# Moving weight loads, U^T loads and six dense blocks around the handover of DK in a fused SSM and dense backward kernel

## The chip, the core and the metric

The kernel runs on one core of a Trainium2 chip. The metric is the device time of one execution in microseconds, as the median of several runs. A NeuronCore has five engines with queues of their own: TensorE (PE, matmuls and transposes, with its weight loads shown apart as PEld), VectorE (DVE), ScalarE (ACT), GpSimd (POOL) and SyncE (SP). SP, ACT and POOL also issue DMA transfers. An engine takes its instructions in the order of its queue; an instruction that waits holds up all that stand behind it there.

## The reference

The kernel computes a forward pass and all its gradients for a gated mix of two branches over one sequence (L = 2048, D = 448):

```python
def _fwd_reference(A_u, ..., B_w1, B_b1, B_w2, B_b2, gate_w):
    x = A_u
    g = _sigmoid((x * gate_w).sum(-1, keepdims=True))
    a = _A_ref(x, A_A_re, ..., A_log_dt, A_Dskip)   # S4: K = Re(sum_n C P dB), y = FFT conv of u with K, + u * Dskip
    b = _B_ref(x, B_w1, B_b1, B_w2, B_b2)           # relu(x w1 + b1)^2 w2 + b2, F = 1792
    return g * a + (1 - g) * b
...
_out, _vjp = jax.vjp(_f, A_u, A_A_re, ..., gate_w)
_grads = _vjp(grad_out)
return (_out, *_grads)
```

The S4 branch's kernel K is a sum over 256 complex modes per channel of powers of exp(dt A) up to 2047, rounded positions included. Its gradient, called DK here, comes from a correlation of u with g * grad_out.

## The kernel before

**Until about 215 us.** The FFT-like stages turn u and g * grad_out into spectra, multiply them, and go back through a first inverse stage (`K.inv1p`), which writes its result to the DRAM scratch `hd[0]`. `K.load_hs(hd[0], q, hss[q], True)` brings it back as four tiles of 128 x 3584 in bf16 (two in tag D16, two in tag P14), with half of the issues on SP and half on ACT. 128 and more small matmuls (L713, weights `Ew`) sum it into DK, held in PSUM tiles N0 to N3 and F.

**The handover of DK.** ACT copies the PSUM tiles to SBUF (L717 to L719). Twelve stores and one for a single row write them to the DRAM scratch `dk_d`, in turns from SP and POOL (L726, L728). Then SP and POOL each reload the whole of DK, once into partitions 0 to 63 and once into 64 to 127 (L733, L735), in the layout that the chunk loop wants. A reload waits for the stores.

**The chunk loop** (`for c in range(NCH + 1)`, 14 chunks of 32 channels, and one round more) builds tables of powers of the modes and uses them in both directions. For chunk c: `seeds_x`, `build_x` and `build_y` (DVE, L773 to L777 and L784 to L787) double tables X and Y step by step, with multipliers that ACT expands (`expand_x`, L807 and L808; `expand_y`, L812 and L814); `kgen` and `k_out` (L844, L852) multiply X and Y into the forward kernel K; `tables_t` and `turn_yt` transpose X and Y through PE, with ACT copies (L871, L883), and `load_yt` does so by DMA for some. `dk_chunk(c)` (ACT, L895 and L896) cuts chunk c's part of DK into `DKs`. In the round after, `back_z(c - 1, ...)` multiplies Y's transposes with `DKs` (L913, "Z", into PSUM tile F, copied by ACT in L917), and `back_p` multiplies Z with X's tables on DVE (L933) and sums with a selection matrix on PE (L942). Tile F has one buffer, so a Z group needs the copy of the one before.

**The dense layers** run beside the loop. `hidden(lb, jp, banks, ring)` computes two blocks of 128 rows of relu(x w1 + b1)^2 for a quarter `lb` of the sequence: eight matmuls (L584, L587) into two PSUM tiles from `banks`, two relus (L589) and a square (L591 or L594) on ACT, and a store of the relu from POOL (L595). Seven `jp` make a quarter. It needs w1 (`w1w`, tag U16, three loads on SP, L697 and L700) and a quarter of U^T (`UTb`, in SB, `load_ut` on POOL, L568). `project` (L1021) multiplies by w2 (`w2n`, tag D16, one load on POOL, L1029) and needs all seven. Then come the transposes of w1 and w2, and `row_block` (L1084 to L1097) for the backward of the dense branch; its products on DVE (L1096) stand in the same queue as the loop's. After the loop K goes through DRAM (`k_d`, `gd[2]`) and the FFT stages for the outputs.

**What sets the order.** The program is written as one text; a scheduler orders each engine's queue at compile time by the place in the text and by when operands are ready in its own model. It may put an instruction ahead of others written before it. Inside `with tc.issue_after(x.ins):` each instruction on x's engine stays behind x in that engine's queue; it does not wait for x's end.

Of the kernel before, what the change touches and what calls it, by code (L numbers as in the profile page):

```python
# [19 lines left out]
P = 128  # L20
L, D, N, F = 2048, 448, 256, 1792
# [313 lines left out]
def kernel(ctx, tc, A_u, A_A_re, A_A_im, A_B_re, A_B_im, A_C_re, A_C_im, A_log_dt, A_Dskip,  # L335
# [3 lines left out]
    nc = tc.nc  # L339
# [6 lines left out]
    def dscr(name, n, dt=bf16):  # L346
        return nc.dram_tensor(name, (n,), dt, kind="Internal")
# [8 lines left out]
    dk_d = dscr("dk_d", 769 * D)  # L356
# [109 lines left out]
    NT = ["N0", "N1", "N2", "N3", "X", "S"]  # L466
# [100 lines left out]
    def load_ut(lb):  # L567
        G_.dma_start(UTb[lb % 2].rearrange("p a l -> p (a l)"), bass.AP(tensor=UT_d, offset=lb * P * 2048, ap=[[2048, P], [1, 2048]]))  # L568

    def hsq(j):  # L570
        return SB[:, 4096 + 512 * j:4608 + 512 * j] if j < 13 else w2v[:, 6272:6784]

    def hidden(lb, jp, banks, ring):
        nonlocal nti, rxi
        ub = UTb[lb % 2]
        rx = ring[rxi % len(ring)]
        rxi += 1
        pss = []
        for j in (2 * jp, 2 * jp + 1):
            ps = K.ps(banks[nti % len(banks)], [P, 512])  # L580
            nti += 1
            pss.append(ps)
            for dt in range(DT - 1):
                T_.matmul(ps[:], lhsT=w1w[:, dt, j * P:j * P + P], rhs=ub[:, dt], start=(dt == 0), stop=False, skip_group_check=True)  # L584
        for k in range(2):
            h, j = slice(64 * k, 64 * k + 64), 2 * jp + k
            T_.matmul(pss[k][:], lhsT=w1w[h, 3, j * P:j * P + P], rhs=ub[h, 3], start=False, stop=True, tile_position=(64 * k, 0), skip_group_check=True)  # L587
        for k in range(2):
            S.activation(rx[:, 512 * k:512 * k + 512], pss[k][:], ACT.Relu, bias=b1_f[:, 2 * jp + k:2 * jp + k + 1])  # L589
        if jp < 6:  # L590
            S.activation(SB[:, 4096 + 1024 * jp:5120 + 1024 * jp], rx, ACT.Square)  # L591
        else:
            for k in range(2):
                S.activation(hsq(12 + k), rx[:, 512 * k:512 * k + 512], ACT.Square)  # L594
        G_.dma_start(bass.AP(tensor=rT_d, offset=2 * jp * P * L + 512 * lb, ap=[[L, P], [P * L, 2], [1, 512]]), rx.rearrange("p (k l) -> p k l", k=2))  # L595
# [96 lines left out]
    for q in range(4):  # L692
        lhs = K.load_hs(hd[0], q, hss[q], True)
    w1v = K.t("U16", [P, 8192])
    w1w = w1v[:, 0:7168].rearrange("p (a f) -> p a f", a=DT)
    with tc.issue_after(lhs.ins):
        nc.sync.dma_start(w1w[:, 0:3], bass.AP(tensor=B_w1.tensor, offset=B_w1.offset, ap=[[F, P], [P * F, 3], [1, F]]))  # L697
    for h in range(2):
        with tc.issue_after(lhs.ins):
            nc.sync.dma_start(w1w[64 * h:64 * h + 64, 3], bass.AP(tensor=B_w1.tensor, offset=B_w1.offset + 384 * F, ap=[[F, 64], [1, F]]))  # L700
    KB = K.t("K28", [P, 14336])
    DK = KB[:, 0:VA * D].rearrange("p (a d) -> p a d", d=D)
    G_.memset(KB[:, 12 * D:VA * D].bitcast(fp32), 0.0)
# [18 lines left out]
    ldk = {}  # L722
    for (a0, na, r0, st_, src) in pieces:
        for al in range(na):
            qe = (nc.sync, G_)[n_ % 2]
            ldk[n_ % 2] = qe.dma_start(bass.AP(tensor=dk_d, offset=(r0 + al) * D, ap=[[st_ * na * D, 16 // st_], [16 * na * D, 4], [1, D]]), src[al::na])  # L726
            n_ += 1
    ldk[n_ % 2] = (nc.sync, G_)[n_ % 2].dma_start(bass.AP(tensor=dk_d, offset=768 * D, ap=[[D, 1], [1, D]]), stB[0:1, 1])  # L728
    for cpy in range(2):
        qe = (nc.sync, G_)[cpy]  # L730
        with tc.issue_after(ldk[cpy].ins):
            for (a0, na, r0, st_, _) in pieces:
                qe.dma_start(DK[64 * cpy:64 * cpy + 64, a0:a0 + na].rearrange("p a d -> p (a d)"),  # L733
                             bass.AP(tensor=dk_d, offset=r0 * D, ap=[[na * D, 64], [1, na * D]]))
            qe.dma_start(DK[64 * cpy:64 * cpy + 1, 12], bass.AP(tensor=dk_d, offset=768 * D, ap=[[D, 1], [1, D]]))  # L735


    YA = K.t("Y16", [P, W2, 2, 64])
# [2 lines left out]
    XWs = [XB[:, 4096 * k:4096 * k + 4096].rearrange("p (t w a r) -> p t w a r", t=2, w=W2, a=NA) for k in range(2)]  # L741
    for k in range(2):
        mx = G_.memset(XB[:, 4096 * k:4096 * k + 4096].bitcast(fp32), 0.0)
    with tc.issue_after(mx.ins):
        load_ut(0)
        load_ut(1)
    Fv = K.t("F17", [P, 8704])
    Vt = Fv[:, 0:4096]
    PRY = Fv[:, 4096:5376].rearrange("p (l w t d) -> p l w t d", l=5, t=2, d=2)
# [43 lines left out]
    def seeds_x(c):  # L793
        V.tensor_copy(XWs[c % 2].rearrange("p t w a r -> p (t w) (a r)")[:, :, 0:4], rx_[c][:, 0:512].rearrange("p (x e) -> p x e", e=4))

    def load_rx(c):
        rx_[c] = K.t("recx", [P, 1024])
        (G_ if c == 1 else nc.sync).dma_start(rx_[c][:], bass.AP(tensor=rec_d, offset=c * P * RS, ap=[[RS, P], [1, 1024]]))
# [17 lines left out]
    def build_x(c):  # L816
        for (s0, st, dst, n, k) in ((0, 1, 2, 2, 0), (0, 2, 4, 2, 1), (0, 4, 6, 2, 2), (0, 4, 8, 2, 3), (6, 1, 10, 3, 3)):
            last = step_x(XWs[c % 2], s0, st, dst, n, k)
        return last
# [66 lines left out]
    def load_yt(c, g):  # L886
        nonlocal yi
        YT = (YTr[yi % 4] if yi % 4 < 3 else P2[:, 2048:4096]).rearrange("p (h i n) -> p h i n", h=2, i=CW)
        yi += 1
        nc.sync.dma_start_transpose(out=YT.rearrange("p h i n -> p (h i) n"), in_=Ys[c % 2][:, 16 * g:16 * g + 16].rearrange("p w t b -> p (w t b)"))  # L890
        return YT
# [6 lines left out]
    def back_z(c, YTs, gs):  # L898

        nonlocal zi  # L900
        cc = c % GC
        DKc = DKs[:, c % 2]
        zb = Zr[zi % 2].rearrange("p (s t g n) -> p s t g n", t=2, s=2, g=2)
        zi += 1
        for gg, g in enumerate(gs):
            psz = K.psF()
            for s in range(2):
                for par in (1, 0):
                    for ii in range(4):
                        i = 2 * ii + par  # L910
                        m = (1 + par) * NA
                        for t in range(2):
                            T_.matmul(psz[32 * ii:32 * ii + m, t, 256 * s:256 * s + 256],  # L913
                                      lhsT=DKc[64 * t:64 * t + 64, s, g, 2 * ii:2 * ii + 1 + par].rearrange("p i a -> p (i a)"),
                                      rhs=YTs[g][64 * t:64 * t + 64, :, i, :], start=True, stop=True, tile_position=(64 * t, 32 * ii),
                                      skip_group_check=True)
            S.copy(zb[:, :, :, gg].rearrange("p s t n -> p t s n"), psz[:].rearrange("p t (s n) -> p t s n", s=2))  # L917
        return zb
# [46 lines left out]
    for c in range(NCH + 1):  # L965
        z01 = z23 = None
        if c < NCH:
            with tc.issue_after(ay.ins) if ay is not None else nullcontext():
                seeds_x(c)
            ax = build_x(c)  # L970
            if c + 1 < NCH:
                load_rx(c + 1)
            XTs[c] = [tables_t(c, 0)]
            YTs[c] = []
        if c > 0:
            z01 = back_z(c - 1, YTs[c - 1], (0, 1))
        if c < NCH:
            XTs[c].append(tables_t(c, 1))
        if c > 0:
            z23 = back_z(c - 1, YTs[c - 1], (2, 3))  # L980
        for half in range(2):
            if c < NCH:
                ay = build_y(c, half, ax if half == 0 else ap or ay)
                if half == 1:
                    k_out(c, kgen(c))
                for g in (2 * half, 2 * half + 1):
                    YTs[c].append(turn_yt(c, g, ("S", "N3")) if c == 0 else turn_yt(c, g) if g == 3 or c == NCH - 1 else load_yt(c, g))
                if c + 1 < NCH:
                    if half == 0:
                        lry = load_ry(c + 1)  # L990
                        lry1 = lry if c == 0 else lry1
                        expand_x(c + 1)
                        if c == 0:
                            expand_y(1, 0, 4)
                    elif c == 0:
                        expand_y(1, 4, 5)
                    else:
                        expand_y(c + 1)
                if half == 0:
                    dk_chunk(c)  # L1000
            ap = None
            if c > 0:
                ap = back_p(c - 1, XTs[c - 1][half], (z01, z23)[half], (2 * half, 2 * half + 1), ay if c < NCH else None)
        if c == 0:
            for jp in range(6):
                hidden(0, jp, NT[4:6], [w1v[:, 7168:8192], Fv[:, 2048:3072], Fv[:, 3072:4096]])

    ring = [w1v[:, 7168:8192], Fv[:, 2048:3072], Fv[:, 3072:4096], P2[:, 0:1024], P2[:, 1024:2048]]
    ni = 0
# [15 lines left out]

    w2v = K.t("D16", [P, 8192])
    w2n = w2v[:, 0:FT * D].rearrange("p (j d) -> p j d", d=D)
    with tc.issue_after(lry1.ins):
        G_.dma_start(w2n, bass.AP(tensor=B_w2.tensor, offset=B_w2.offset, ap=[[D, P], [P * D, FT], [1, D]]))  # L1029
    hidden(0, 6, NT[0:3], ring)  # L1030
    for lb in range(4):
# [410 lines left out]
```

## Time and profile before

| | us |
|---|---|
| Median of 5 runs (lowest, highest) | 951.65 (943.29, 961.45) |
| Profiled execution, own time | 951.03 |
| Its span, first to last instruction | 948.9 |
| Granted TensorE clock, mean | 0.841 of full |

| Stretch, us | What runs | DVE busy | ACT busy | PE busy |
|---|---|---|---|---|
| 209 to 236 | DK's last sums and handover; chunk 1's tables | 19.5 | 13.4 | 17.6 |
| 236 to 263 | first Z, hidden of the first quarter | 12.0 | 26.0 | 22.5 |
| 316 to 342 | one chunk in the middle of the loop | 25.3 | 21.2 | 21.2 |
| 650 to 700 | after the loop | 16.5 | 19.9 | 37.6 of 50 |

Times in the profile are microseconds from the start of the span. In a line of the timeline stand start, duration, engine, line, operation, output and input tile; in square brackets the idle time of the engine before it and what ended that. In the list of waits stand the time in all, how often, and the longest. In the DMA issues stand the size of one and the median time from issue to landing.

### The profile page before, as it was taken

How to read it: one execution, taken by the hardware profiler on the slowest of the kernel's cores; microseconds unless marked ns; L12 is line 12 of the kernel's file. 1: busy time of each engine (PE TensorE's matmuls, PEld its weight loads, DVE VectorE, ACT ScalarE, POOL GpSimd, SP SyncE). 2: the span in 40 equal slices, each digit the busy share in tenths (PEclk: the TensorE clock that was granted, in tenths of full speed). 3: DMA queues.
4: the chain of work that ended last, by engine and by line, in shares of the span. 5: the costliest groups of instructions: out<-in, count | busy, mean ns of one | idle time of the engine just before them, and what ended most of it. 6: DMA issues, size and time to landing. Idle time of an engine off the chain costs nothing. (4 is left out here: it accounts for less than half of the span.)

```text
span 948.9 us, 19001 instructions
## 1 busy us (share of the span) xinstructions
PE 709.3 (75%) x7657; PEld 341.7 (36%) x7657; DVE 671.0 (71%) x1152; ACT 587.0 (62%) x936; POOL 191.8 (20%) x327
## 2 busy tenths in 40 slices
PE   3335574636978888887898887988968789767975
PEld 1112221214344443433463442543323245423443
DVE  4388985696399999999987899845249571297700
ACT  3346757825998868788776764655337636437543
POOL 2141000112202121121211311232300022433310
PEclk9677665767969998999958997989979979868998
DMA  9987385796626667445844776379989994879431
GB/s 190 261 246 266 128 341 232 300 313 195 148 59 128 152 141 140 107 106 120 193 89 122 217 156 160 90 186 284 383 300 283 297 290 134 236 225 282 146 107 44
DMA packets 161887, 184.98 MB, mean 195 GB/s; under 512 B 90963, under 2 KB 137464, under 8 KB 160872
## 3 DMA queue, kind: packets, MB, share of 16 engines
q1 hardware_dynamic: 111958, 82.38, 35.3%
q0 software_dynamic: 20480, 61.51, 20.1%
q10 hardware_dynamic: 29362, 39.88, 12.7%
q8 instruction: 60, 0.98, 0.4%
q14 instruction: 27, 0.22, 0.1%
HBM read 90.58 MB, written 73.13 MB: 173 GB/s over the span
## 5 line engine op out<-in xcount | busy, mean ns | idle before, releaser
L933 DVE TENSOR_TENSOR P<-R 128x2048 bf16<-128x2048 bf16 x42 | 49.5, 1218 | 24.2 <-ACT R L917 20.8
L1159 PEld LDWEIGHTS <-S 128*128 128x128 bf16 x448 | 43.8, 103 | 61.3 <-issue 18.4
L917 ACT CAST R<-psF 128x1024 bf16<-128x1024 f32 x56 | 57.3, 1024 | 13.3 <-PE psF L913 13.3
L1021 PE MATMUL psN<-D,S 128*128 128x448 bf16 x208 | 50.5, 374 | 6.4 <-ACT S L591 6.3
L1159 PE MATMUL psF<-U,S 128*128 128x448 bf16 x224 | 50.4, 374 | 2.4 <-ACT S L1154 2.4
L584 PE MATMUL psN<-S,U 128*128 128x512 bf16 x132 | 41.5, 434 | 8.8 <-ACT F L589 4.4
L913 PE MATMUL psF<-R,S 64*32 64x256 bf16 (+1 forms) x1344 | 38.6, 302 | 10.5 <-DMA R<-Y 4.2
L1084 PE MATMUL psN<-S,U 128*128 128x512 bf16 x126 | 39.1, 432 | 6.9 <-ACT D L1089 6.9
L773 DVE TENSOR_TENSOR X<-X,F 128x512 bf16<-128x512 bf16 (+1 forms) x70 | 37.5, 536 | 4.5 <-ACT F L807 2.6
L784 DVE TENSOR_TENSOR K<-K,F 128x2048 bf16<-128x2048 bf16 (+3 forms) x42 | 36.4, 866 | 5.1 <-ACT F L812 3.5
L1153 PEld LDWEIGHTS <-S 128*128 128x128 bf16 x448 | 29.6, 102 | 27.0 <-issue 10.1
L207 DVE CAST K<-psN 128x448 bf16<-128x448 f32 x36 | 21.6, 620 | 24.8 <-PE psN L255 24.6
L785 DVE TENSOR_TENSOR F<-K,F 128x2048 bf16<-128x2048 bf16 (+3 forms) x42 | 35.9, 854 | 3.3 <-ACT F L814 3.3
L1097 POOL DMA_DIRECT2D dhT_d<-D x28 | 20.1, 720 | 88.8 <-DVE D L1096 88.5
L784 DVE TENSOR_TENSOR Y<-Y,F 128x2048 bf16<-128x2048 bf16 (+3 forms) x42 | 36.3, 864 | 1.6
L787 DVE TENSOR_TENSOR K<-K,F 128x2048 bf16<-128x2048 bf16 (+3 forms) x42 | 36.4, 866 | 1.3
L774 DVE TENSOR_TENSOR F<-X,F 128x512 bf16<-128x512 bf16 (+1 forms) x70 | 36.9, 527 | 0.6
L787 DVE TENSOR_TENSOR Y<-Y,F 128x2048 bf16<-128x2048 bf16 (+3 forms) x42 | 36.3, 865 | 1.3
L785 DVE TENSOR_TENSOR F<-Y,F 128x2048 bf16<-128x2048 bf16 (+3 forms) x42 | 35.9, 855 | 0.3 <-ACT F L814 0.3
L1021 PE MATMUL psN<-S,D 128*128 128x448 bf16 x168 | 35.7, 361 | 0.0
L1354 DVE SCALAR_TENSOR_TENSOR F<-psN,Y 128x448 bf16<-128x448 f32 x16 | 9.9, 617 | 36.4 <-PE psN L329 36.4
L913 PEld LDWEIGHTS <-S 64*16 64x16 bf16 (+1 forms) x1792 | 22.4, 91 | 34.5 <-issue 26.7
(378 smaller groups left out, 1942.8 us busy)
## 6 DMA issues: line engine op xcount, KB each, us to landing
sp<-K ACTq DMA_DIRECT2D x8, 896.0 KB, 5.8
hd<-st ACTq DMA_DIRECT2D x16, 448.0 KB, 3.2
dhT_d<-D POOLq DMA_DIRECT2D x28, 256.0 KB, 5.3
R<-sp SPq DMA_DIRECT2D x8, 896.0 KB, 9.9
S<-rT_d POOLq DMA_DIRECT2D x14, 512.0 KB, 5.3
R<-hd SPq DMA_DIRECT2D x16, 448.0 KB, 6.7
S<-dhT_d POOLq DMA_DIRECT2D x14, 512.0 KB, 4.6
rec_d<-F ACTq DMA_DIRECT2D x2, 1920.0 KB, 9.1
```

Source lines behind the costliest of these rows:

```text
L584: T_.matmul(ps[:], lhsT=w1w[:, dt, j * P:j * P + P], rhs=ub[:, dt], start=(dt == 0), stop=False, skip_group_check=True)
L773: V.tensor_tensor(out=hi4, in0=lo, in1=bcast_dims(pr, [0, (None, n), 1]), op=ALU.mult)
L774: V.tensor_tensor(out=Vv.rearrange("p (x a r) -> p x a r", x=2 * W2, r=2), in0=lo, in1=bcast_dims(pi, [0, (None, n), 1]), op=ALU.mult)
L784: V.tensor_tensor(out=hi, in0=lo, in1=bcast_dims(pr, [0, (None, n // 2), 1]), op=ALU.mult)
L785: V.tensor_tensor(out=Vv.rearrange("p (x a q) -> p x a q", x=rows, q=2), in0=lo, in1=bcast_dims(pi, [0, (None, n // 2), 1]), op=ALU.mult)
L787: return V.tensor_tensor(out=T4[:, :, :, n:2 * n], in0=T4[:, :, :, n:2 * n], in1=V4, op=ALU.add)
L913: T_.matmul(psz[32 * ii:32 * ii + m, t, 256 * s:256 * s + 256], lhsT=DKc[64 * t:64 * t + 64, s, g, 2 * ii:2 * ii + 1 + par].rearrange("p i ...
L917: S.copy(zb[:, :, :, gg].rearrange("p s t n -> p t s n"), psz[:].rearrange("p t (s n) -> p t s n", s=2))
L933: lastp = V.tensor_tensor(out=pr.rearrange("p s t g n -> p s t (g n)"), in0=zv, in1=(xb if r == 0 else rev_dim(xb, 2)), op=ALU.mult)
L1021: lastm = T_.matmul(ps[:, 0:D], lhsT=hblk[j][:, P * tt:P * tt + P], rhs=ws[:, j, :], start=(w == 1 and j == 0), stop=(j == FT - 1))
L1084: T_.matmul(ps[:], lhsT=w2Tw[:, jp, dt, j % 2], rhs=dblk[:, dt], start=(dt == 0), stop=False, skip_group_check=True)
L1159: lastm = T_.matmul(ps[:, 0:width], lhsT=hh[:, t, :], rhs=(DB2[:, t, :] if w == 0 else U[:, t, 0:D + 1]), start=(t == 0), stop=(t == LT - 1))
```

## The change

Five edits. The three loads of w1 stand behind SP's last store of DK instead of behind the last load of `hd[0]`; the two loads of U^T stand behind POOL's last store of DK instead of behind a memset of X's buffers; the load of w2 stands behind POOL's last reload of DK instead of behind the load of chunk 1's Y record. `dk_chunk(0)` is written in the second half of chunk 0's round, not the first (the other chunks' stay). The six calls `hidden(0, 0)` to `hidden(0, 5)` are written in round c = 1, behind both `back_z` of chunk 0, instead of at the end of round c = 0, and use PSUM tiles N0, N1, N2 in place of X and S.

```diff
@@ -693,11 +693,6 @@
     w1v = K.t("U16", [P, 8192])
     w1w = w1v[:, 0:7168].rearrange("p (a f) -> p a f", a=DT)
-    with tc.issue_after(lhs.ins):
-        nc.sync.dma_start(w1w[:, 0:3], bass.AP(tensor=B_w1.tensor, offset=B_w1.offset, ap=[[F, P], [P * F, 3], [1, F]]))
-    for h in range(2):
-        with tc.issue_after(lhs.ins):
-            nc.sync.dma_start(w1w[64 * h:64 * h + 64, 3], bass.AP(tensor=B_w1.tensor, offset=B_w1.offset + 384 * F, ap=[[F, 64], [1, F]]))
...
     ldk[n_ % 2] = (nc.sync, G_)[n_ % 2].dma_start(bass.AP(tensor=dk_d, offset=768 * D, ap=[[D, 1], [1, D]]), stB[0:1, 1])
+    with tc.issue_after(ldk[0].ins):
+        nc.sync.dma_start(w1w[:, 0:3], bass.AP(tensor=B_w1.tensor, offset=B_w1.offset, ap=[[F, P], [P * F, 3], [1, F]]))
+        for h in range(2):
+            nc.sync.dma_start(w1w[64 * h:64 * h + 64, 3], bass.AP(tensor=B_w1.tensor, offset=B_w1.offset + 384 * F, ap=[[F, 64], [1, F]]))
+    with tc.issue_after(ldk[1].ins):
+        load_ut(0)
+        load_ut(1)
     for cpy in range(2):
...
-            qe.dma_start(DK[64 * cpy:64 * cpy + 1, 12], bass.AP(tensor=dk_d, offset=768 * D, ap=[[D, 1], [1, D]]))
+            lrk = qe.dma_start(DK[64 * cpy:64 * cpy + 1, 12], bass.AP(tensor=dk_d, offset=768 * D, ap=[[D, 1], [1, D]]))
...
-    with tc.issue_after(mx.ins):
-        load_ut(0)
-        load_ut(1)
...
             z23 = back_z(c - 1, YTs[c - 1], (2, 3))
+        if c == 1:
+            for jp in range(6):
+                hidden(0, jp, NT[0:3], [w1v[:, 7168:8192], Fv[:, 2048:3072], Fv[:, 3072:4096]])
         for half in range(2):
...
-                if half == 0:
+                if half == (1 if c == 0 else 0):
                     dk_chunk(c)
...
-        if c == 0:
-            for jp in range(6):
-                hidden(0, jp, NT[4:6], [w1v[:, 7168:8192], Fv[:, 2048:3072], Fv[:, 3072:4096]])
...
-    with tc.issue_after(lry1.ins):
+    with tc.issue_after(lrk.ins):
         G_.dma_start(w2n, bass.AP(tensor=B_w2.tensor, offset=B_w2.offset, ap=[[D, P], [P * D, FT], [1, D]]))
```

## The prediction

> **What bounds the kernel now.** I read the busy table first, then the windows around the change, then the waits of VectorE (DVE) and ScalarE (ACT) there, the timeline, and last the DMA issues. The busy table says only that TensorE and VectorE are both near three quarters.
>
> ```profile
> PE 709.3 (75%) x7657; PEld 341.7 (36%) x7657; DVE 671.0 (71%) x1152; ACT 587.0 (62%) x936; POOL 191.8 (20%) x327
> ```
>
> The windows show where which engine counts.
>
> ```profile
> core 0: us, PE busy (x) PEld busy (x) DVE busy (x) ACT busy (x) POOL busy (x), PEclk, DMA share, GB/s
> 209.00:236.00 27.00, 17.56 (x297) 12.59 (x298) 19.51 (x33) 13.41 (x21) 8.05 (x14) 0.83 0.75 221
> 236.00:263.00 27.00, 22.46 (x283) 9.95 (x284) 12.04 (x12) 26.04 (x38) 4.91 (x7) 0.91 0.63 145
> 316.00:342.00 26.00, 21.17 (x356) 10.76 (x339) 25.28 (x39) 21.21 (x31) 3.47 (x6) 0.93 0.60 138
> 498.00:524.00 26.00, 21.47 (x230) 8.46 (x208) 19.84 (x24) 18.69 (x27) 5.09 (x9) 0.83 0.54 134
> ```
>
> A chunk of the loop takes 26 us, and DVE is busy for 25.3 of them: the loop goes at DVE's pace. Only where the loop starts (236 to 263) does DVE work 12 of 27 us; there ACT is full (26.0) and PE nearly so. Later, at 498, DVE waits again, on the dense layers. The waits of DVE and ACT between 209 and 260 name the holes:
>
> ```profile
> DVE P L933 <- ACT R L917: 12.9, 1, 12.9
> ACT S L895 <- DMA K<-dk_d: 5.5, 1, 5.5
> DVE K L784 <- ACT F L812: 3.5, 1, 3.5
> DVE F L785 <- ACT F L814: 3.3, 1, 3.3
> ```
>
> The timeline tells their story:
>
> ```profile
> 233.97 0.89 ACT L895 COPY S<-K 128x416 bf16<-128x416 bf16 x1 [5.50 <-DMA K<-dk_d]
> 236.09 1.23 DVE L784 TENSOR_TENSOR K<-K,F 128x2048 bf16<-128x2048 bf16 x1 [3.49 <-ACT F L812]
> 242.17 0.69 ACT L589 ACTIVATE U<-psX,b_f 128x512 bf16<-128x512 f32 x1
> 245.93 1.04 ACT L917 CAST R<-psF 128x1024 bf16<-128x1024 f32 x1
> 251.52 1.07 ACT L917 CAST R<-psF 128x1024 bf16<-128x1024 f32 x1
> 252.63 2.36 DVE L933 TENSOR_TENSOR P<-R 128x2048 bf16<-128x2048 bf16 x2 [12.92 <-ACT R L917]
> ```
>
> ACT stands at dk_chunk(0) (L895) until DK has landed; behind it in ACT's queue stand expand_y(1, 4, 5) and the copies of turn_yt, and DVE waits 3.5 us for the first. Then PE and ACT alternate between the hidden blocks (L584, L589, L591) and the first Z (L913, L917): two Z copies are 5.6 us apart, and DVE gets its first product 12.9 us late. The DMA issues of 188 to 240 show why DK lands at 233.9:
>
> ```profile
> P<-hd SPq DMA_DIRECT2D x2, 448.0 KB, 15.1
> U<-in_B_w_dram SPq DMA_DIRECT2D x2, 224.0 KB, 16.2
> D<-in_B_w_dram POOLq DMA_DIRECT2D x1, 1568.0 KB, 14.9
> S<-UT_d POOLq DMA_DIRECT2D x2, 512.0 KB, 4.2
> ```
>
> The loads of hd, which DK's matmuls need, take 15 us while U^T, w1 and w2 share the DMA engines (share 1.02 in 193.7 to 213.4, at 318 GB/s).
>
> **The change, part by part.**
>
> *Loads moved behind DK's stores.* In 193.7 to 213.4 the engines moved 19.7 x 318 = 6.26 MB, of which hd is 8 x 448 KB = 3.67 MB and recx and recy 0.49 MB; 2.1 MB are U^T and parts of w1 and w2. Without them hd lands after 4.16 / 318 = 13.1 us, 6.6 us earlier; with U^T's 1.05 MB alone taken out it would be 3.3. I take 6. The last matmuls of L713 (213.4 to 216.3), the copies (to 218.5) and the stores (to 220.5) follow, so the stores end at 214.5. The moved issues cost SP 0.41 + 2 x 0.49 = 1.4 us and POOL 1.05 us between stores and reloads, where both queues wait anyway (SP 3.4 and POOL 4.8 us on the stores' landing): nothing. If that cover were gone, the reloads would be up to 1.4 us later. U^T also leaves POOL's place ahead of recx and recy of chunk 1; those loads may come about 1 us earlier, with nothing waiting for them but expand_x(1), whose time I leave alone.
>
> *DK's reload.* From the stores' end to the reload's landing it took 233.9 - 220.5 = 13.4 us. Now w1 and U^T (2.62 MB) are on the same queues ahead of the reload (1.38 MB): 4.0 MB at the 301 GB/s of 213.4 to 220.5 are 13.3 us, the same. So DK lands at about 228. Bounds: 224.5 if the reload isn't held at all (4 us for the stores, 6 for the reload), 237 if the three go one after the other (4 + 2.62 / 0.301 = 8.7 + 9.9). I take 228, since the gap at 222 to 226, where the share fell to 0.36, is there for w1.
>
> *w2 behind DK's reload instead of recy(1).* It goes from 208.65 to about 222, landing by its row some 15 us later, 237. Who waits: project(0), first at 245 in this profile, and it needs all of hidden first. Cost nothing; the cover is 8 us.
>
> A page of the Trainium skill speaks against all three: "DMA: Bandwidth & Descriptors", section "Rules for kernel authors", wants a load issued early and waited for late, to hide its fixed cost. By it moving weights back costs their exposure, and the sum would lose what PE waits for w1, up to the 15 us of the third rival below. The row above speaks the other way: a third of what moved while hd was loaded was loads not needed yet. The same page's "Queues, rings and completion order" has descriptors of one ring taken in order, which would put SP's reload wholly behind w1; no run here shows that, and by it DK would land near the late end, 237.
>
> *dk_chunk(0) in the second half, not the first.* ACT now does expand_y(1, 4, 5) and the four turn_yt copies first. DVE's 3.5 us wait goes, and it reaches its first product at 239.7 - 3.5 = 236.2. What is late next: Z itself. From DK's landing: two ACT operations (0.89 + 0.99), then twice 1.0 us of L913 and 1.04 of L917: 228 + 6 = 234 to 235. So the first product starts at about 237 instead of 252.6; with DK at 237 it would be 243.5.
>
> *hidden(0, 0 to 5) behind chunk 0's Z, in banks N0 to N2.* In 236 to 260 these blocks took PE 9.53 (L584) + 2.94 (L587) = 12.5 us and ACT 7.82 (L589) + 6.69 (L591) = 14.5 us, just where DVE stood still. The work isn't removed. It now stands ahead of expand_x(2) on ACT: four operations which got a slot about every 2.8 us among hidden's. DVE's L774 of chunk 2, at 263.3 before, comes after L773 at 237 + 6.2 = 243.2 and two products, so at 246 if ACT is free, and at 250 if the four slots last until 239 + 11. I take 250: a gain of 13 at that point, between 17 (ACT free) and 6 (DK late as well). The 3.3 us at L785 came from PE's waiting on w1 in hidden(0, 6); that wait may go or grow. I count zero, from -3 to + what the third rival says.
>
> *What of the 13 us reaches the end.* Up to 446 the loop has 97% of DVE's time in it, so a lead is kept. At 466 to 550 DVE waits for the dense layers (5.9 + 2.5 us at L1096). If the dense work came later by all its 12.5 us of PE, the lead would be gone; PE has 26 - 22.1 = 3.9 us idle in each of some seven chunks before, 27 us, which take that up. Behind the loop the way goes by k_out, k_d and gd (DMA share 1.0 in 650 to 700), and PE stands after the last row block, at 686 to 692 and 693 to 697, for loads that would come with the loop. I count 2 us lost, between 0 and 10.
>
> **Sum.** Own time of the profiled execution 951.03 (span 948.9 and 2.1 outside it): 951.03 - 13 + 2 = 940.0. The median of the runs is 951.65, within 0.6 of it. Taken from the bounds of each step, this case spans 932 to 947.
>
> **Rivals.**
>
> *Given back in the dense phase.* The loop starts 13 us earlier, but at L1096 waits 10 us longer, because the dense layers keep their time: 951 - 3 = 948. For it: PE at 85% in the loop and at a granted clock of 0.51 in 472 to 498. Against it: dense work too was held up at the start (hidden(0, 6)'s relu came only at 276.8).
>
> *The order isn't what the text says.* Instructions are ordered by a scheduler by priority and readiness; hidden(0, 6), written far behind, already ran at 217.9. If the early blocks again go into PE's queue ahead of Z, because w1 and U^T are there before DK, only the 3.5 us at L784 go: 947.5.
>
> *PE waits for w1 (slower).* One place: hidden's first matmul in PE's queue, at 217.2 before. If it stays there and w1, issued at 215 to 216, takes its row's 16.2 us, PE stands until 232. Behind it are the X transposes, the Y transposes and K's matmuls. ACT's L871 and with it L814 come 10 us later, DVE's L785 goes from 224.8 to 235, turn_yt ends at 251, Z at 255 instead of 251.5; hidden then falls on chunk 1 and keeps expand_x(2) until 270 instead of 263.3: +7, 958. It decides from some 13 us of standing on; below that it only eats the gain. For it: PE already waited 2.5 us for w1 here. Against it: the scheduler sees the later issue and should place the block later.
>
> **How the numbers follow.** Forecast 0.60, given back 0.15, order 0.07, PE waits 0.18. The predicted time is the forecast's, 940.0. The range of 8 in 10 goes from 931 (the forecast with L785's 3 us as well, less a little) to 957, short of the slow rival's 958 and beyond. About 1% is what a measurement of this kernel tells from no change, 942.1 and 961.2 around the median; I count the slow rival as slower, as it has no end at 958. Faster: 0.7 of the forecast's 0.60 and 0.03 from elsewhere, 0.45. Slower 0.18 less what lies within, 0.15. Within: 0.40.
>
> **What would show it.** Right: hd landing near 207, DK's stores over by 215, L895 without a DMA wait or landing near 228; L917's first pair ahead of the early L589; DVE's first L933 at 235 to 240; chunk 2's L774 near 250; loop windows unchanged at 25 of 26. Wrong: a wait of PE on U<-in_B_w_dram above 5 us near 217 to 235; L913 still between the L584 of hidden(0, 0 to 5); or L1096's wait near 505 grown by as much as the start gained.

## Result and the profile after

The changed kernel takes 954.20 us (median of 44 runs, 949.01 to 962.67); beside it the kernel before took 951.74 (median of 79). The ratio is 1.004, with a 95% interval of 1.0024 to 1.0055: 2.5 us were lost where 11 were forecast as gained. All ratios, here and below, leave out the runs more than 1.5% above their kernel's lowest; of e4_hold_hidden below that takes six of twelve, so its ratio lies below what its median says. The profiled execution took 956.26, with a span of 954.2, against 951.03 and 948.9 before. The busy table shows that no work was added:

```profile
PE 712.9 (75%) x7657; PEld 344.4 (36%) x7657; DVE 671.3 (70%) x1152; ACT 586.4 (61%) x936; POOL 192.4 (20%) x327
```

In the changed kernel most line numbers are lower by one: Z's product on DVE is L932 (before L933), the copy of Z L916, expand_y L813, dk_chunk L894, turn_yt L881 and L882; DK's sums are L708 (before L713). The windows:

```profile
core 0: us, PE busy (x) PEld busy (x) DVE busy (x) ACT busy (x) POOL busy (x), PEclk, DMA share, GB/s
209.00:236.00 27.00, 12.40 (x155) 8.53 (x148) 21.63 (x35) 10.87 (x18) 9.45 (x16) 0.69 0.73 194
236.00:263.00 27.00, 23.09 (x363) 13.48 (x363) 10.87 (x10) 22.25 (x31) 2.88 (x4) 0.83 0.72 158
316.00:342.00 26.00, 22.46 (x372) 11.04 (x370) 24.91 (x38) 24.94 (x34) 4.21 (x7) 0.93 0.75 162
498.00:524.00 26.00, 21.47 (x345) 11.81 (x344) 19.81 (x33) 17.43 (x23) 6.20 (x10) 0.70 0.27 80
```

Between 209 and 236 PE worked 12.4 us instead of 17.6, and ACT 10.9 instead of 13.4. In the next window DVE still works 11 of 27 us: the hole that the change was to close is as wide as before. Waits of DVE, ACT and PE between 205 and 270 give its cause:

```profile
PE psN L584 <- DMA U<-in_B_w_dram: 11.1, 1, 11.1
ACT R L882 <- PE psN L881: 11.5, 1, 11.5
DVE F L784 <- ACT F L813: 5.8, 1, 5.8
DVE P L932 <- ACT R L916: 13.6, 1, 13.6
DVE X L772 <- ACT F L806: 4.8, 1, 4.8
```

These are links of one chain, in the order of the lines, as the timeline shows:

```profile
218.86 0.37 SPq L723 DMA_DIRECT2D dk_d<-st  x1
219.33 0.42 SPq L725 DMA_DIRECT2D U<-in_B_w_dram  x1
221.25 3.50 SPq L735 DMA_DIRECT2D K<-dk_d  x5
233.97 1.03 PE L584 MATMUL psN<-S,U 128*128 128x512 bf16 x2 [11.10 <-DMA U<-in_B_w_dram]
235.90 1.01 ACT L882 COPY R<-psN 128x1024 bf16<-128x1024 bf16 x1 [11.54 <-PE psN L881]
237.35 1.23 DVE L784 TENSOR_TENSOR F<-K,F 128x2048 bf16<-128x2048 bf16 x1 [5.83 <-ACT F L813]
246.25 0.91 ACT L894 COPY S<-K 128x416 bf16<-128x416 bf16 x1
252.40 1.05 ACT L916 CAST R<-psF 128x1024 bf16<-128x1024 f32 x1
253.48 2.36 DVE L932 TENSOR_TENSOR P<-R 128x2048 bf16<-128x2048 bf16 x2 [13.64 <-ACT R L916]
```

In PE's queue the first two matmuls of hidden still stand ahead of chunk 0's Z: in the middle of its turn_yt, and ahead of most of kgen. w1 is issued at 219.3 and there at 234.0, and from 222.9 until then PE stands. Behind those two matmuls are the rest of turn_yt; ACT waits for it at L882, and behind that copy on ACT stands expand_y (L813), for which DVE waits, and then dk_chunk(0). Its copy of DK (L894) no longer waits for a DMA, because it starts only at 246.3 (before: 234.0). The first product comes at 253.5, 0.9 us later than before. The DMA issues from 188 to 250 show what the handover became:

```profile
D<-hd SPq DMA_DIRECT2D x2, 448.0 KB, 6.8
S<-UT_d POOLq DMA_DIRECT2D x2, 512.0 KB, 5.7
K<-dk_d POOLq DMA_DIRECT2D x4, 112.0 KB, 8.1
U<-in_B_w_dram SPq DMA_DIRECT2D x2, 224.0 KB, 16.4
K<-dk_d SPq DMA_DIRECT2D x4, 112.0 KB, 19.2
```

The two reloads of DK are alike but for their queues. POOL's, behind U^T, lands after 8.1 us, and SP's, behind w1, after 19.2. (The stores ahead of them gained: 56 KB landed in 2.1 us from SP and 1.9 from POOL, where before it took 6.9 and 7.0.)

At the far end, the last matmul of the last row block stands on PE, first before and then after:

```profile
673.22 0.81 PE L1084 MATMUL psS<-S,U 128*128 128x512 bf16 x3
```

```profile
680.84 0.81 PE L1083 MATMUL psS<-S,U 128*128 128x512 bf16 x3
```

It is 7.6 us later; the span grew by 5.3. In all the kernels below, from this matmul to the span's end it took 273 to 279 us.

### The profile page after: what moved, and what is told of

Same layout as the page of the kernel before. It is cut to its first block, busy times and chain, and to the rows that moved or that the text cites. A ratio compares the mean times of both kernels' runs of the same rounds, so it can differ in the third digit from the quotient of the medians.

```text
span 954.2 us, 19004 instructions
## 1 busy us (share of the span) xinstructions
PE 712.9 (75%) x7657; PEld 344.4 (36%) x7657; DVE 671.3 (70%) x1152; ACT 586.4 (61%) x936; POOL 192.4 (20%) x327
## 3 DMA queue, kind: packets, MB, share of 16 engines
q10 hardware_dynamic: 29362, 39.88, 12.9%
## 4 chain that ended last, share of the span: by engine, by line
issue 26%; PE 23%; DMA 16%; ACT 15%; DVE 10%; POOL 6%; SPq 2%; ACTq 1%; POOLq 0%; DVEq 0%
PE psN L1020 4%; PE psF L1158 3%; DMA S<-rT_d 2%; POOL dhT_d L1096 2%; SPq L422 2%; PE psN L584 2%; ACT R L916 2%; DMA hd<-st 1%; ACT S L591 1%; PE psX L843 1%; DMA R<-K 1%; DMA U<-in_A_u_dram 1%; DMA S<-dhT_d 1%; DMA D<-hd 1%; PE psF L912 1%
## 5 line engine op out<-in xcount | busy, mean ns | idle before, releaser
L584 PE MATMUL psN<-S,U 128*128 128x512 bf16 x168 | 51.4, 420 | 20.9 <-DMA U<-in_B_w_dram 11.1
L932 DVE TENSOR_TENSOR P<-R 128x2048 bf16<-128x2048 bf16 x42 | 49.6, 1218 | 23.6 <-ACT R L916 19.4
L916 ACT CAST R<-psF 128x1024 bf16<-128x1024 f32 x56 | 57.6, 1028 | 13.7 <-PE psF L912 13.5
L1020 PE MATMUL psN<-D,S 128*128 128x448 bf16 x208 | 53.3, 394 | 4.7 <-ACT S L591 4.7
L912 PE MATMUL psF<-R,S 64*32 64x256 bf16 (+1 forms) x1344 | 36.3, 296 | 11.3 <-DMA R<-Y 4.1
L1083 PE MATMUL psN<-S,U 128*128 128x512 bf16 x126 | 37.2, 415 | 6.9 <-ACT D L1088 6.9
L784 DVE TENSOR_TENSOR F<-K,F 128x2048 bf16<-128x2048 bf16 (+3 forms) x42 | 35.9, 855 | 5.8 <-ACT F L813 5.8
L1096 POOL DMA_DIRECT2D dhT_d<-D x28 | 20.2, 723 | 89.5 <-DVE D L1095 89.2
L773 DVE TENSOR_TENSOR F<-X,F 128x512 bf16<-128x512 bf16 (+1 forms) x70 | 36.9, 526 | 1.6 <-ACT F L807 1.0
L882 ACT COPY M<-psX 128x1024 bf16<-128x1024 bf16 x26 | 26.7, 1027 | 15.6 <-PE psX L881 15.5
L784 DVE TENSOR_TENSOR F<-Y,F 128x2048 bf16<-128x2048 bf16 (+3 forms) x42 | 35.9, 855 | 0.4 <-ACT F L813 0.4
```

What stands on the lines that cost most here:

```text
L784: V.tensor_tensor(out=Vv.rearrange("p (x a q) -> p x a q", x=rows, q=2), in0=lo, in1=bcast_dims(pi, [0, (None, n // 2), 1]), op=ALU.mult)
L932: lastp = V.tensor_tensor(out=pr.rearrange("p s t g n -> p s t (g n)"), in0=zv, in1=(xb if r == 0 else rev_dim(xb, 2)), op=ALU.mult)
L1020: lastm = T_.matmul(ps[:, 0:D], lhsT=hblk[j][:, P * tt:P * tt + P], rhs=ws[:, j, :], start=(w == 1 and j == 0), stop=(j == FT - 1))
L1083: T_.matmul(ps[:], lhsT=w2Tw[:, jp, dt, j % 2], rhs=dblk[:, dt], start=(dt == 0), stop=False, skip_group_check=True)
L1096: G_.dma_start(bass.AP(tensor=dhT_d, offset=2 * p_ * P * L + 512 * lb, ap=[[L, P], [P * L, 2], [1, 512]]), hb)
```

## Experiments

One table first, as every experiment is read from it. "First product" is the first L933 (L932), "chunk 3" the first of its seeds on DVE; both are counted from the seeds of chunk 1 (212 to 217 in the span), which run ahead of what the edits reach on DVE, so that what a run had lost before then is left out. "Row block" is the start of the last line of matmuls shown above, in the span. These three columns come from one profiled run each. Single runs of one kernel vary by about 1% either way, so a profile's own time, and a few us in the last of the three, are no measure: e3 and e11 have the median of the kernel before, but their profiled runs lie 6 us below it and reach the row block 4 us ahead of the profile of before. The ratio is to the runs of the kernel before on the same chip.

| Kernel | First product | Chunk 3 | Row block | Median us | Ratio (95%) |
|---|---|---|---|---|---|
| before | +39.6 | +77.4 | 673.2 | 951.74 | 1 |
| after | +39.4 | +81.3 | 680.8 | 954.20 | 1.0040 (1.0024 to 1.0055) |
| e1_w1_early | +31.9 | +73.4 | 671.0 | 951.57 | 0.9980 (0.9941 to 1.0019) |
| e2_loads_only | +41.9 | +79.7 | 683.3 | 959.94 | 1.0082 (1.0050 to 1.0114) |
| e3_order_only | +31.7 | +71.1 | 668.9 | 952.25 | 0.9993 (0.9957 to 1.0029) |
| e4_hold_hidden | +37.8 | +80.9 | 666.3 | 951.96 | 0.9929 (0.9881 to 0.9978) |
| e5_dk_first | +31.2 | +74.3 | 667.4 | 943.01 | 0.9907 (0.9869 to 0.9945) |
| e6_order_hold | +32.7 | +77.2 | 672.0 | 947.04 | 0.9931 (0.9899 to 0.9963) |
| e7_w2_later | +36.9 | +81.3 | 684.9 | 957.74 | 1.0067 (1.0029 to 1.0105) |
| e8_dve_delay | +41.0 | +78.8 | 682.3 | 958.91 | 1.0056 (1.0021 to 1.0090) |
| e9_hold_bp | +31.2 | +66.4 | 671.0 | 946.65 | 0.9930 (0.9891 to 0.9969) |
| e10_warm | +28.7 | +72.0 | 671.0 | 947.79 | 0.9959 (0.9925 to 0.9994) |
| e11_dk_only | +39.3 | +77.1 | 668.8 | 952.24 | 1.0013 (0.9980 to 1.0046) |

The time of e4 is read as between no change (its median) and -0.7% (its ratio).

### The cause: w1 late for a queue that takes things in order

**e1_w1_early** is the changed kernel with the three w1 loads where they were before.

```diff
+    with tc.issue_after(lhs.ins):
+        nc.sync.dma_start(w1w[:, 0:3], ...)          # w1's three loads, behind hd's
...
-    with tc.issue_after(ldk[0].ins):
-        nc.sync.dma_start(w1w[:, 0:3], ...)          # the same three
```

> The changed kernel with one part undone: the three loads of w1 stand behind the loads of hd again; U^T and w2 stay late, dk_chunk(0) and the hidden blocks stay where the change put them. Theory (TensorE's queue stands 11.1 us at hidden's first matmul because w1 now lands at 234): the wait on U<-in_B_w_dram falls from 11.1 to under 3 us, DVE's wait of 5.8 us at expand_y(1, 4, 5) goes, the first Z product on DVE starts at 236 to 242 instead of 253.5, and the time falls by 6 to 12 us below the changed kernel, to 942 to 948. Rival (the new place and banks of the hidden blocks cost the time, whatever the loads do): 952 to 957, with the gap on DVE ahead of the first Z product gone but a gap as long later in chunk 1.

PE's wait for w1 is gone; what is left is a wait of 3.4 us for U^T at the same matmul. DVE's wait of 5.8 for expand_y's second part is gone, and the first product comes 7.5 us earlier. In the list of waits of e1:

```profile
PE psN L584 <- DMA S<-UT_d: 3.4, 1, 3.4
DVE P L933 <- ACT R L917: 11.6, 1, 11.6
DVE P L933 <- PE psN L942: 3.6, 1, 3.6
```

The order of DVE and POOL is the same as in the changed kernel, so the slowdown is w1's: with its load back the ratio is 0.998, and the interval lies wholly below that of the changed kernel. But the forecast's gain isn't there either: the time is that of before, within an interval that leaves room for 5.6 us, and above the 942 to 948 expected.

**e2_loads_only** and **e3_order_only** split the change in two: the kernel before with the loads of w1, U^T and w2 moved and nothing else, and with dk_chunk(0) and the six calls of hidden moved and nothing else.

```diff
 # e2: as in the change
+    with tc.issue_after(ldk[0].ins):  ...  # w1
+    with tc.issue_after(ldk[1].ins):  load_ut(0); load_ut(1)
+    with tc.issue_after(lrk.ins):  ...  # w2
 # e3: as in the change
+        if c == 1:
+            for jp in range(6): hidden(0, jp, NT[0:3], ...)
+                if half == (1 if c == 0 else 0):
```

> The kernel before with the three moves of loads alone (w1, U^T and w2 late as in the change); dk_chunk(0) and the hidden blocks stand where they stood before. Theory: the wait for w1 in TensorE's queue is there without the other two edits, 8 to 13 us, and as dk_chunk(0) still stands ahead of expand_y(1, 4, 5) on ScalarE, DVE waits for DK's reload as well, which now lies behind w1: the first Z product at 256 to 262, time 955 to 960. Rival (the loads are a gain, the dense blocks' place is the loss): first Z product before 250, 944 to 949.

> The kernel before with the two moves in the text alone: dk_chunk(0) in the second half of chunk 0 and hidden(0, 0 to 5) behind chunk 0's Z in banks N0 to N2; all loads stand where they stood before. Theory: no wait for w1 above 3 us, DK lands at 232 to 235 as before, DVE's 3.5 us at L784 go, and the first Z product starts at 239 to 243 instead of 252.6: time 941 to 947. Rival (the place of the hidden blocks is the loss): 952 to 957.

The loads alone cost 0.8%. In e2's waits PE stands for w1 and DVE longer than ever for its first product:

```profile
PE psN L584 <- DMA U<-in_B_w_dram: 9.3, 1, 9.3
ACT R L882 <- PE psN L881: 9.8, 1, 9.8
DVE P L932 <- ACT R L916: 20.4, 2, 18.7
```

e2 came as expected. The order alone does what the prediction said of it at the start, at a smaller size: DVE's wait at Z falls from 12.9 to 7.5, and the first product is 7.9 us earlier.

```profile
DVE P L933 <- ACT R L917: 7.5, 1, 7.5
```

None of that is seen in the time, which was expected at 941 to 947 (the ratio's interval leaves room for 4 us). So both halves failed, each in its own way.

**e11_dk_only**, the kernel before with dk_chunk(0) alone moved, takes the order apart once more.

```diff
-                if half == 0:
+                if half == (1 if c == 0 else 0):
                     dk_chunk(c)
```

> This is the kernel before with dk_chunk alone moved to the second half of chunk 0's back_z; loads and early blocks stay where they were. The prediction counted 3.5 us for this move, as VectorE's wait at L784. Theory A (the wait was on the path): it falls below 1.5 us, the first Z product comes at about 249 instead of 252.6, and the time is 2 to 3.5 us below that of before. Theory B (the wait's place is taken by the next one in the same chain): the first Z product comes at 251.5 to 253 and the time is within 1.5 us of before.

DVE's wait of 3.5 at L784 is gone, but the first product comes where it came before, and its wait took over the 3.5: 12.9 before, now

```profile
DVE P L933 <- ACT R L917: 17.8, 2, 16.0
DVE F L785 <- ACT F L814: 3.2, 1, 3.2
```

That is theory B: the 3.5 us were in a chain that had slack until Z's copy. What brings the first product forward in e3 is the six blocks of hidden.

**e7_w2_later** asks whether w1 is late because w2 and the rest share the DMA engines with it, or by its own transfer: in the changed kernel, w2's load waits behind hidden's first store.

```diff
-    with tc.issue_after(lrk.ins):
+    with tc.issue_after(hs0.ins):        # hs0: the store of hidden(0, 0)
         G_.dma_start(w2n, ...)
```

> The changed kernel with w2's load moved once more, behind the first store of a hidden block on GpSimd's queue, so that it does not share the DMA engines with w1; the order on TensorE, ScalarE, VectorE and SyncE is that of the changed kernel. Theory (w1 takes 15 us because U^T, DK's reloads and w2 share the way): TensorE's wait for w1 falls from 11.1 to 6 to 9 us and the time by as much as 2 to 5, to 949 to 952. Rival (w1's own transfer sets it): wait 10.5 to 11.5, time 953 to 955.

```profile
PE psN L584 <- DMA U<-in_B_w_dram: 9.5, 1, 9.5
```

PE's wait fell only from 11.1 to 9.5, which lies between the two theories, and the time didn't fall (0.0027 above the changed kernel's ratio, within the intervals). So most of w1's lateness is not w2's doing.

### What can be had: DK first, the blocks held

**e4_hold_hidden** is the changed kernel with the order that its text asks for made binding on PE: hidden(0, 0) to (0, 6) stay behind chunk 0's last Z matmul.

```diff
+                            K.lastz = T_.matmul(psz[32 * ii:32 * ii + m, t, 256 * s:256 * s + 256], ...)
...
+            lz = K.lastz
+                with tc.issue_after(lz.ins):
                     hidden(0, jp, NT[0:3], ...)
```

> The changed kernel with all seven hidden blocks of the first quarter held behind the last matmul of chunk 0's Z in TensorE's queue; the loads stay late. Theory: the wait for w1 moves out of the way of chunk 0's transposes and of K's matmuls, so expand_y(1, 4, 5) comes without DVE's 5.8 us; what is left is SP's reload of DK, which lies behind w1 and lands at 238 to 243: first Z product at 244 to 249, time 945 to 951. Rival (the late loads cost nothing once hidden is out of the way): first Z product before 240, 940 to 945. Rival (the dense blocks' place is the loss): 954 or more.

PE no longer waits for w1. What was hidden behind that wait comes out: DK itself. The list of waits and the DMA issues of e4:

```profile
DVE P L932 <- ACT R L916: 17.9, 1, 17.9
ACT S L894 <- DMA K<-dk_d: 10.9, 1, 10.9
```

```profile
K<-dk_d POOLq DMA_DIRECT2D x4, 112.0 KB, 8.3
U<-in_B_w_dram SPq DMA_DIRECT2D x2, 224.0 KB, 15.9
K<-dk_d SPq DMA_DIRECT2D x4, 112.0 KB, 17.4
```

ACT gets DK at 246.0, 12 us later than before the change, because SP's reload lies behind w1. That is 3 us later than the latest expected, and the first product, at 253.0, 4.

**e5_dk_first** adds one thing to e4: w1 is issued behind SP's reload of DK and U^T behind POOL's, not between the stores and the reloads.

```diff
-    with tc.issue_after(ldk[0].ins):   # w1 behind SP's last store
-    with tc.issue_after(ldk[1].ins):   # U^T behind POOL's last store
...
+    with tc.issue_after(lr0.ins):      # w1 behind SP's last reload
+    with tc.issue_after(lrk.ins):      # U^T behind POOL's last reload
```

> The changed kernel, all seven hidden blocks of the first quarter held behind chunk 0's Z on TensorE, and the loads of w1 and U^T behind DK's reloads instead of between stores and reloads, so that nothing but w2 shares the way with DK. Theory A (the lead of the first Z product reaches the end, less 2 or 3 us): DK lands at 226 to 231, first product at 236 to 239 (15 us before the kernel before), time 937 to 943. Theory B (the lead is given back where the displaced hidden blocks come, and in the dense layers): same first product, but chunk 3 starts no more than 6 us ahead of the kernel before (290.5) and the time is 947 to 953.

```profile
K<-dk_d POOLq DMA_DIRECT2D x4, 112.0 KB, 2.7
K<-dk_d SPq DMA_DIRECT2D x4, 112.0 KB, 4.9
```

The same reload lands in 4.9 us instead of 17.4; dk_chunk(0) starts at 229.2, and the first product at 244.9 is 7.7 us earlier than before the change. At 943.01 us and a ratio of 0.9907 (0.9869 to 0.9945) this version beats both kernels. DK landed as expected, but the first product came 6 us later than expected, and chunk 3 has a lead of only 3.2 us: the time is theory A's, the small lead is theory B's sign. So the start need not be where this gain arises; see what stays open.

**e6_order_hold** has e5's order of instructions on ACT and DVE and all but the same on PE, and the loads where they were before the change. It tells how much of e5 is order.

```diff
+    with tc.issue_after(lhs.ins):  ...  # w1 behind hd's loads, as before
+    with tc.issue_after(mx.ins):        # U^T behind the memset, as before
+        load_ut(0)
+        load_ut(1)
+    with tc.issue_after(lry1.ins):  ... # w2 as before
```

> The order of e5 on every engine, with all loads where the kernel before has them. DK lands at 232 to 235; first product at 239 to 242. Theory A: 3 to 4 us behind e5, 941 to 947. Theory B: the same time as e5 within its interval, 947 to 953.

Most of it is: 0.9931 against 0.9907, with DK at 236.7 instead of 229.2 (1.7 us later than expected; the first product, at 247.9, 6). The intervals overlap, so the loads' share (4 us by the medians, 2 by the ratios) is not settled. It shows that moving the loads is at best a small gain, and only behind the reload. And chunk 3 of e6 starts at +77.2, where it started before the change (+77.4): e6 gains 0.7% with no lead there at all.

### Where the lead at the start goes

**e8_dve_delay** puts 8 us of extra copies on DVE at chunk 3 of the kernel before, to see whether the loop's place counts at the end.

```diff
-                seeds_x(c)
+                for _ in range(29 if c == 3 else 1):
+                    seeds_x(c)
```

> The kernel before, with the seeds' copy of chunk 3 done 29 times instead of once: 8 us of work on VectorE in the middle of the loop, nothing else. If VectorE's chain sets the end (theory A), the time is 957 to 960. If the dense layers take up a shift of the loop (theory B), 951 to 954.

The loop's last copy of Z comes 8.8 us later (648.9), the last row block 9.0, the span 6.7, and the ratio says 5.3 us (2.0 to 8.6). So a lag on DVE does reach the end, by about two thirds, give or take as much as 3 us.

**e9_hold_bp** is e5 with the blocks held one step further, behind the first half of back_p.

```diff
-                    with tc.issue_after(lz.ins):          # behind chunk 0's Z
+                lz = K.lastbp                             # behind back_p's first half
+                    with tc.issue_after(lz.ins):
                         hidden(0, jp, NT[0:3], ...)
```

> This is e5_dk_first with the early blocks of the first dense layer held back further on TensorE: behind the first half of back_p of round 1 instead of behind the first chunk's Z products. In e5 VectorE still stands 7.1 us for back_p's products, which come behind 20 matmuls of hidden in TensorE's queue. Theory A (TensorE's queue order around the handover is what decides): that wait goes or falls below 3 us, the seeds of chunk 2 come about 4 us earlier than e5's 260.2, and the time is 937 to 941. Theory B (a lead at the handover is given back in the dense phase, where the blocks held back are then late): the seeds of chunk 2 come earlier all the same, but the time is within 2 us of e5's 943.0. Theory C (the blocks held back run into UT's late use): seeds of chunk 2 not earlier, time 943 to 947.

At the start it works as wished. In e5 DVE waited twice, in e9 once (both lists of DVE's waits from 205 to 270, e5 first):

```profile
DVE P L933 <- ACT R L917: 9.7, 1, 9.7
DVE P L933 <- PE psN L942: 7.1, 1, 7.1
```

```profile
DVE P L933 <- ACT R L917: 11.4, 1, 11.4
```

Chunk 3 starts 7.9 us earlier than in e5. Of that, 3.2 us are left at chunk 13, and the time is no better (946.65 against 943.01, intervals overlapping). That comes nearest to theory B, although the time is 1.6 us outside its 2. Theory B's reason, that the blocks held back are late in the dense layers, isn't shown: the last group of hidden's matmuls at L584 starts 8.6 us later on PE (443.6 against 435.0), but the quarter's last relu on ACT only 0.7 us (446.3 against 445.6), and a last row block at 671.0 against 667.4 is within what single profiles differ by.

**e10_warm** tests another piece of the start. In the changed kernel DK's sums (L708) ran at half the clock:

```profile
core 0: us, PE busy (x) PEld busy (x) DVE busy (x) ACT busy (x) POOL busy (x), PEclk, DMA share, GB/s
196.00:201.50 5.50, 0.00 (x0) 0.00 (x0) 4.83 (x12) 2.40 (x4) 0.55 (x1) 0.50 1.02 221
201.50:210.00 8.50, 7.32 (x77) 3.53 (x81) 8.33 (x9) 0.00 (x0) 0.00 (x0) 0.50 1.04 312
210.00:218.00 8.00, 5.74 (x99) 3.64 (x92) 7.72 (x14) 4.55 (x9) 2.68 (x6) 0.93 0.18 48
```

So e10 gives PE 44 matmuls of no use ahead of the sums in e5.

```diff
+    psW = K.ps("X", [P, 512])
+    with tc.issue_after(K.last_i1.ins):
+        for _ in range(44):
+            T_.matmul(psW[:], lhsT=ident[:], rhs=ct["Etw"][:, 0:512], start=True, stop=True)
```

> This is e5_dk_first with 44 extra matmuls of 128x512 on TensorE, ahead of the sums that make DK; their result is used nowhere. In the changed kernel the sums ran from 201.6 to 210.5 at a granted clock of 0.50, so that hd's landing 6 us earlier brought the last sums only 1.3 us (215.0 against 216.3). Theory A (the half clock swallowed the gain): the sums run at a clock above 0.7, the last cast of DK starts by 211 to 212, DK's stores end by 216, the first Z product comes 2 to 4 us earlier than in e5 (244.9), and the time is 2 to 4 us below e5's 943.0. Theory B (the sums wait for hd's landing, not for the clock): their end stays within 1 us of 215.0 and the time within 1.5 us of e5's.

```profile
core 0: us, PE busy (x) PEld busy (x) DVE busy (x) ACT busy (x) POOL busy (x), PEclk, DMA share, GB/s
196.00:198.00 2.00, 1.78 (x9) 0.59 (x6) 1.93 (x5) 0.00 (x0) 0.00 (x0) 1.00 0.75 151
202.00:206.00 4.00, 3.81 (x40) 1.78 (x44) 3.83 (x9) 0.00 (x0) 0.55 (x1) 0.50 1.06 343
208.00:212.00 4.00, 2.72 (x46) 1.60 (x42) 3.93 (x4) 0.65 (x2) 0.00 (x0) 1.00 0.57 158
```

The clock rose with the filler, fell again in the 4.2 us that PE then stood for hd, and was full from about 207.4 on, some 2 us earlier than in e5 (209.6). The sums didn't end earlier for it, as they now waited for the last part of hd (at 212.3). The test isn't clean, since hd's loads were issued 1.4 us later in this run (195.8 against 194.4). The three casts behind the sums start at 215.2 (e5: 214.3), the seeds of chunk 2 at 261.1 (260.2), and the ratio is 0.9959. So theory A isn't borne out: the clock rose, and the sums met hd's landing instead. The time is above what either theory gave.

## Why the prediction was wrong, step by step

The step that failed is the place of `hidden`: the sum has the blocks behind chunk 0's Z and no wait of PE for w1. PE stood 11.1 us for it, with the rest of turn_yt and kgen behind (e1 takes that wait away, and the loss with it; e2 has the loss without the order). That explains the 2.5 us lost. That the 11 us of gain aren't there in e1 and e3 either is for the steps below.

**hd 6 us earlier, stores over by 214.5: mis-sized.** The stores' last issue is at 218.9 instead of 220.2, a gain of 1.3. Two things stand against the rest; the second, the clock, is argued, as e10 doesn't settle it. The division by 318 GB/s held the rate fixed: with w1 and U^T gone, the DMA engines stayed full (share 1.02) but moved only 221 GB/s in 196 to 201.5, where before they moved 301; the share fell only at 210, 3.4 us ahead of the last wait for hd before (213.4). And before, the clock of the sums had risen at 206.6, and they then waited for hd (0.8 and 1.6 us); now they ran at 0.50 until past 210.5 and had no such waits, only one of 1.05 us early on (at 204.9). The same windows before the change:

```profile
196.00:201.50 5.50, 0.00 (x0) 0.00 (x0) 4.92 (x12) 1.37 (x3) 0.54 (x1) 0.50 1.04 301
201.50:210.00 8.50, 5.84 (x81) 3.10 (x84) 8.33 (x9) 1.14 (x2) 1.11 (x1) 0.71 1.06 348
```

**DK lands at 228, within 224.5 to 237: wrong, and outside its bounds.** e4, where ACT waits for DK itself, has it at 246.0. Stores 4.7 us later than counted shift the late bound to 241.7. The rest is not accounted for by a run; w2's 1.6 MB were on the way too and are not in the sum. What failed is "13.3 us, the same": it took the four megabytes as one pool, shared by all, and SP's reload took 17.4 us behind w1 and 4.9 us ahead of it (e4, e5), POOL's only 8.3 in the same e4. Two readings were off besides: by the DMA issues w1 and U^T are 2.88 MB and not 2.62 (the sum would give 14.2 us), and the share in 222 to 226 is 0.43 and not 0.36.

The prediction had a rule in hand for this: the Trainium skill, "DMA: Bandwidth & Descriptors", section "Queues, rings and completion order", has descriptors of a ring taken in order. POOL's 8.1 against SP's 19.2 us in one run, and e4 against e5, agree with it. The prediction set it aside because no run had shown it.

**The 3.5 us at L784: wrong as a gain.** e11 takes that wait away and the first product doesn't move (+39.3, before +39.6): it was slack ahead of Z's copy.

**First product at 237, chunk 2's L774 at 250 instead of 263.3: wrong.** The first product is at 253.5, and that line of chunk 2 (now L773) at 268.3, 5.0 us later than before instead of 13 earlier; its seeds came 3.3 us later. In e5, with both mistakes of the change mended, the first product is at 244.9 and the seeds of chunk 2 are still not earlier (260.2 against 258.4), because DVE then waits 7.1 us for back_p behind hidden's matmuls: the prediction had no such wait. In e9, with the blocks held behind it, that wait is gone and the seeds are at 253.1.

**A lead kept up to 446 and 2 us lost after: wrong in one direction.** A lag is kept (e8: 5.3 of 8 us; the changed kernel and e2). A lead isn't: e3 and e9 start chunk 3 by 6.3 and 11.1 us earlier than before, and the time of e3 is that of before (at most 4 us less), and of e9 no better than e5's, whose lead is 3.2 us. Already at chunk 8, inside the loop, 2.7 of e3's 6.3 us are left (seeds at +213.5, before +216.1). So the first rival, "given back in the dense phase", isn't shown either: the wait that it named, at L1096 in 450 to 550, is 8.9 us in e3 and was 8.4 before.

**w2 at no cost: holds.** No engine waits for w2's load in the changed kernel, and e7 moves it away and gains nothing.

**The third rival was the right one**, "PE waits for w1", held at 0.18. It named the place (hidden's first matmul in PE's queue), a wait on U<-in_B_w_dram above 5 us as its sign, and the chain over ACT to expand_y. Its sizes: PE stood 11.1 us (from 222.9 to 234.0), not 14.8; chunk 2 came 5.0 us later, not 7; and the time rose by 2.5 and not by 7. What stood behind the matmul was turn_yt and kgen, not the transposes of X. It lost in the weighing by one sentence: "the scheduler sees the later issue and should place the block later". It did place it later, behind half of turn_yt instead of among the transposes of X, but by its own model of the transfer, and w1 landed 11 us after its place in the queue.

**What stays open.** Where the 0.7 to 0.9% of e5, e6 and e9 arise isn't settled, and the start is the less likely place. e3 leads by 6.3 us at chunk 3 and gains at most 0.4%; e6 leads by 0.3 and gains 0.7% (0.4 to 1.0). What all kernels with held blocks share (e4, e5, e6, e9, e10) is another order behind chunk 9, since the scheduler re-arranged the rest of the loop when the blocks were held: of the 28 products of the row blocks on DVE (L1096), 14 stand ahead of chunk 13's seeds before, in the changed kernel and in e3, but 11 in e4, e5 and e6 and 10 in e9. Counted from chunk 1's seeds, those of chunk 9 come at +245.1 before, +242.1 in e5, +246.8 in e6 and +250.0 in e4, and those of chunk 13 at +375.9, +365.1, +367.2 and +368.7. A part of this is only products put behind; how much of it is time gained, no run shows, as none has the later order without the held blocks.

## What to carry to other kernels

A load that is moved back has to be checked against the first instruction that needs it in the queue as it is really ordered, not in the text, and everything behind that instruction pays. Hold the consumer (`issue_after`) in the same edit that delays its load, and then look at the whole queue again, far behind the place of the edit too: here the hold also changed the order 250 us later. When an urgent small transfer and a big patient one go through one queue, put the urgent one first: with 1.8 MB of w1 ahead of it DK's reload took 17.4 us, ahead of w1 4.9. And removing one wait near a join says nothing by itself: ask which chain arrives next, in the dense layers as well as in the loop.

## What the runs showed of the hardware

The DMA engines showed a share of 1.02 at 221 GB/s (after, 196 to 201.5) and of 1.06 at 348 GB/s (before, 201.5 to 210): the share says that they are occupied, not how much they move, so bytes taken off a full stretch didn't shorten it in proportion here.

After an idle stretch TensorE's granted clock was 0.50 for very different times: in DK's sums 3.3 us before the change (203.3 to 206.6), 9 us after it (from 201.6 to past 210.5, with a wait of 1.05 us within), 5.5 us in e10 (201.9 to 207.4). The Trainium skill, "TensorE: Matmul & The Clock Gate", Part 1, gives about 3.4 us of steady work to the full clock; the row of before agrees with it, and the other two took longer; whether the short wait in the stretch is the reason, no run here shows.
